# Top-k attention and a SmeLU MLP on one core: where ScalarE's copy of a chunk's MLP sum stands in the order

## The chip, the core and the metric

The kernel runs on one core of one Trainium2 chip. The metric is the device time of the whole program in microseconds (us): 1482.36 is the median of three runs, 1481.56 to 1483.75. The core's engines each have their own queue of instructions and work through it in order: TensorE (PE in the profile, with PEld for its weight loads), VectorE (DVE), ScalarE (ACT), GpSimd (POOL), and SyncE (SP), whose queue issues the transfers (DMA). Engines wait for one another by semaphores.

## The reference

Attention over 8 batches, 8 heads, 576 positions and head size 64, in which each row keeps only its 32 largest scores; its output goes, heads side by side, as 4608 rows of 512 into an MLP with 2048 hidden units.

```python
scores = scale * np.matmul(q, k.transpose(0, 1, 3, 2))
kth = np.partition(scores, -top_k, axis=-1)[..., -top_k:-top_k + 1]
scores = np.where(scores >= kth, scores, -1000000000.0)
attn = softmax(scores)                      # exp(scores - max) / (sum + 1e-09)
x = np.matmul(attn, v)                      # then (B,H,S,D) -> (B*S, H*D)

h = x @ w_in
g = np.where(h >= 1, h, np.where(h <= -1, 0.0, (h + 1) ** 2 / 4))
out = g @ w_out
```

All numbers are float32.

## The kernel before

**Attention in steps.** The work is cut into 144 steps; a step is 128 query rows of two heads. In a step TensorE makes the scores `sp` (line 358) and ScalarE copies them, scaled, to `s` (L359). VectorE finds the 32nd largest of each row: it folds the row in two halves, the pairwise larger and smaller ones (`more`, `less`, L372), and runs MAX8 and MATCH_REPLACE8 over them (L379 to L446); `kth` is the result (L451). ScalarE makes the exponentials `e` (L395) with the negated row maximum `nmax` (L393); VectorE masks and sums them (L458), and GpSimd divides them by their sum (L411, with VectorE's reciprocal `rz`, L404). The weights are then transposed: early and in the last steps by TensorE (`pw`, `pwt`, L473 and L479, with a diagonal matrix `diag` that ScalarE makes, L408), and in all other steps by way of DRAM: ScalarE splits the words into 16-bit `halves` (L488), SyncE writes them out as `rows` (L490) and a transposing transfer brings them back as `wT` (L492). TensorE multiplies with the values (`po`, L506 or L514) and ScalarE copies the outcome into `xT` (L519 or L521). Keys and queries are turned in the same two ways; on the way through DRAM ScalarE's part is `parts` (L283) and SyncE's are `lines<-parts` (L285) and a transposing transfer (L292).

**The MLP in chunks.** A chunk is 128 rows of `xT`; there are 36, one after every four steps, counted from 0 in what follows. For each chunk TensorE makes 8 hidden groups of 256 units (`ph`, L539, eight matrix products each; the last chunk has 16 groups of 128) and, from the activated `g`, 16 final products that are summed in one PSUM tile, `py` (L578). Of `py` there is one buffer, so the first final product of a chunk, which begins a new sum, has to wait until the old sum has been read. ScalarE makes `r` and `g` of each hidden group (L550, L558), and GpSimd finishes `g` (L565 to L568); in the last chunk VectorE does that (L554, L555). After the 16th final product ScalarE copies `py`, scaled, to `y` (L581) and SyncE sends `y` to the output (L583). In the profile each matrix product of the MLP shows as two records: a hidden group as 16, a final product as 2.

**Who sets the order.** The order of instructions on TensorE, VectorE, ScalarE and GpSimd is the order in which the program hands them out: a manual schedule is opened before the first step and closed after the last. Every step has 7 places (`slot`), in each of which VectorE's next part, and if they are due ScalarE's, GpSimd's and TensorE's other parts, are handed out. MLP work sits in a list `pending` and is taken by a budget of TensorE's time (`advance`, `take`). The last 8 final products of a chunk are put behind the first three hidden groups of the next. Two things are already handed out later than they are made: the readings of hidden groups (`reads`) and GpSimd's part of them (`bounds`). The order on SyncE is not written by hand; it is chosen when the program is built.

**Around a hand-over** from one chunk to the next, in nearly all chunks, TensorE has: the old chunk's last final product, three hidden groups of the new chunk, the new chunk's first final product, then scores and `po`. Before the change ScalarE has `y` straight after what was handed out before the last final product.

Of the kernel before, what the change touches and what calls it, by code (L numbers as in the profile page):

```python
# [11 lines left out]
F32 = mybir.dt.float32  # L12
# [14 lines left out]
def kernel(  # L27
# [10 lines left out]
    nc = tc.nc  # L38
# [3 lines left out]
    P = 128  # L42
# [134 lines left out]
    def run(ctx, paired):  # L177
# [352 lines left out]
        def mlp(xT, rows, pool, last):  # L530
            gs, group, whole_g = {}, 1 if last else GROUP, set()
            py = []

            def hidden(x):
                ph = ps.tile([P, group, P], F32, name="ph", tag="ph", bufs=3)
                for i in range(group):
                    f = x * group + i
                    for kk in range(NK):
                        nc.tensor.matmul(ph[:, i], w_in[:, kk, f * P:(f + 1) * P], xT[:, kk],  # L539
                                         start=(kk == 0), stop=(kk == NK - 1))  # L540

                reads.append(partial(read, x, ph))
                if not holding:
                    issue_reads()

            def read(x, ph):
                while len(bounds) > 1:
                    bounds.popleft()[1]()
                r = pool.tile([P, GROUP, P], F32, name="r", bufs=2)[:, 0:group]
                nc.scalar.activation(r, ph, AF.Relu, bias=half, scale=0.5 * unit)  # L550
                gs[x] = g = pool.tile([P, GROUP, P], F32, name="g", bufs=2 * LAG)[:, 0:group]
                if last:
                    nc.scalar.activation(g, ph, AF.Relu, bias=minus_half, scale=0.5 * unit)
                    nc.vector.scalar_tensor_tensor(out=r, in0=r, scalar=1.0, in1=r, op0=ALU.min, op1=ALU.mult)  # L554
                    nc.vector.tensor_tensor(out=g, in0=r, in1=g, op=ALU.add)  # L555
                    whole_g.add(x)
                    return
                nc.scalar.activation(g, ph, AF.Relu, bias=minus, scale=unit)  # L558
                by_act = converted < n_pieces and x % 2
                if by_act:  # L560
                    nc.scalar.activation(r, r, AF.Square)
                bounds.append((slots_done, partial(bound, x, r, g, by_act)))

            def bound(x, r, g, by_act):
                nc.gpsimd.tensor_scalar(r, r, 1.0, 0.0, ALU.min, ALU.max)  # L565
                if not by_act:
                    nc.gpsimd.tensor_tensor(out=r, in0=r, in1=r, op=ALU.mult)  # L567
                nc.gpsimd.tensor_tensor(out=g, in0=r, in1=g, op=ALU.add)  # L568
                whole_g.add(x)

            def final(f):
                if f == 0:
                    py.append(ps.tile([P, DM], F32, name="py", tag="py", bufs=1))
                if f // group not in gs:
                    issue_reads()
                while f // group not in whole_g:
                    bounds.popleft()[1]()
                nc.tensor.matmul(py[0], gs[f // group][:, f % group], w_out[:, f, :], start=(f == 0), stop=(f == NF - 1))  # L578
                if f == NF - 1:
                    y = (late or words).tile([P, DM], F32, name="y", bufs=1)  # L580
                    nc.scalar.activation(y, py[0], AF.Copy, scale=unit)  # L581
                    for p0, p1, dst in rows:
                        nc.sync.dma_start(out=dst, in_=y[p0:p1])  # L583

            behind = []
            while pending and pending[-1][3]:
                behind.insert(0, pending.pop())
            for x in range(NF // group + LAG):  # L590
                if x < NF // group:
                    pending.append((NK * group, needed(x * group + group - 1, False), partial(hidden, x), False))
                if x < LAG:
                    for _ in range(min(GROUP + 1, len(behind))):
                        pending.append(behind.pop(0)[0:3] + (False,))
                else:
                    for f in range((x - LAG) * group, (x - LAG + 1) * group):
                        pending.append((DM // P, needed(f, True), partial(final, f), x >= NF // group))
# [22 lines left out]
        total, spent = len(chunks) * (NK * NF + NF * DM // P), 0  # L621
        converted, inspected, due = 0, 0, 0.0

        reads, bounds, holding, slots_done = [], deque(), False, 0

        def issue_reads():
            while reads:
# [138 lines left out]
        for m in range(n + 2):  # L766
# [22 lines left out]
            for slot in range(SLOTS):  # L789
                now = start + (dve_time - start) * (slot + 1) / SLOTS  # L790
                for _ in range(parts[slot]):
                    next(top_k, None)
                if m < n and converted < n_pieces:
                    if slot in now_converting:
                        convert(now)
                elif slot == 3 and late is not None:
                    if m % 2:
                        inspect()
                    elif paired:
                        load(late, inspected, 1, 2)  # L800
                if slot == 1 and 1 <= m <= n and state[m - 1]["by_tensor"]:
                    pe_time = max(pe_time, done[m - 1] + 2.0) + 1.0
                    transpose_w(state[m - 1])
                    ready_at[m - 1] = pe_time + 1.8
                if slot == 3 and 1 <= m <= n and state[m - 1] is not None and not state[m - 1]["by_tensor"]:
                    move_w(state[m - 1])
                    ready_at[m - 1] = done[m - 1] + 15.0
                if slot == 3:
                    finish_turns()
                if slot == 2 and m == n and paired:  # L810
                    judge(ps, att)
                if slot == 2 and (early or m == first_late or m >= n - 1):
                    values_until(m)
                if m == 0 and slot in (1, 2):
                    next(first)
                holding = not early and m % 2 == 0 and slot in (1, 2) and m < n
                if slot == 2 and not early:
                    if m % 2 == 0:
                        while len(reads) < 3 and pending and taken is not None and taken.__name__ == "hidden" and take():
                            pass  # L820
                    begin_until(min(m + 2, len(state)))
                    holding = False
                    issue_reads()
                    values_until((m - 2) // 2 * 2)
                    begin_until(m + 3 - m % 2)
                if slot == 4 and early:
                    begin_at(m + 2)
                if slot == (6 if early else 1):
                    queries(m + (3 if early else 5))
                    if (m < n and prep is None and next_keys < B and steps[m][0] == next_keys - 1 and steps[m][1] >= 1  # L830
                            and (next_keys > 1 or converted == n_pieces)):
                        prep = (turned_keys_of if next_keys > 1 else keys_of)(next_keys)
                    if prep is not None and (m % 2 == 0 or next_keys == 1):
                        got = next(prep, None)
                        pe_time += 0.5 if next_keys < 2 else 0.0
                        if got is None:
                            prep, next_keys = None, next_keys + 1
                        else:
                            keys[next_keys] = got
                            value_loads = got.get("loads", value_loads)  # L840
                    elif value_loads is not None:
                        next(value_loads, None)
                if paired and early and spent == 0 and not pending:
                    rest = ps.tile([P, NT, P], F32, name="rest", tag="py", bufs=1)
                    for i in range(5):
                        nc.tensor.transpose(rest[:, i % NT, :], ident, ident)
                advance((EARLY_SHARE if early else share) / SLOTS if m < n else 32.0, now)
                slots_done += 1
                while bounds and (early or m >= n or bounds[0][0] < slots_done - 2):
                    bounds.popleft()[1]()  # L850
            for _ in (top_k if top_k is not None else ()):
                pass
        while pending:
            advance(32.0, pe_time + 8.0)
            while bounds:
                bounds.popleft()[1]()
        order.__exit__(None, None, None)


# [45 lines left out]
```

## Time and profile before

| What | Value |
|---|---|
| Median of the timed runs | 1482.36 us |
| Profiled execution: its time, its span | 1484.11 us, 1482.2 us |
| TensorE's clock granted, mean | 0.992 |
| TensorE busy | 1435.8 us, 97% |
| VectorE busy | 1403.9 us, 95% |
| ScalarE busy | 1158.0 us, 78% |
| GpSimd busy | 926.6 us, 63% |
| `y` (L581) | 36 times, 583 to 604 ns, median 597 |
| Transfer of `y` (L583) | 40 issues, to landing 3.7 us (median) |

The profile is of one execution, whose span is the time from its first to its last instruction; what lies around the span is the rest of its time. "Busy" counts time in which an engine works, not waits. In timelines each line has start, duration, engine, line of the kernel, operation, what it writes `<-` what it reads, and sizes; a bracket at the end gives the time for which the engine was idle just before, and what ended it. Ends of TensorE's products in the profile are modelled, so two that follow each other can overlap there by a tenth or two. VectorE's and GpSimd's durations contain whatever blocked them after their start.

### The profile page before, as it was taken

How to read it: one execution, taken by the hardware profiler on the slowest of the kernel's cores; microseconds unless marked ns; L12 is line 12 of the kernel's file. 1: busy time of each engine (PE TensorE's matmuls, PEld its weight loads, DVE VectorE, ACT ScalarE, POOL GpSimd, SP SyncE). 2: the span in 40 equal slices, each digit the busy share in tenths (PEclk: the TensorE clock that was granted, in tenths of full speed). 3: DMA queues.
4: the chain of work that ended last, by engine and by line, in shares of the span. 5: the costliest groups of instructions: out<-in, count | busy, mean ns of one | idle time of the engine just before them, and what ended most of it. 6: DMA issues, size and time to landing. Idle time of an engine off the chain costs nothing.

```text
span 1482.2 us, 32086 instructions
## 1 busy us (share of the span) xinstructions
PE 1435.8 (97%) x10755; PEld 1044.6 (70%) x10755; DVE 1403.9 (95%) x4392; ACT 1158.0 (78%) x2221; POOL 926.6 (63%) x1310
## 2 busy tenths in 40 slices
PE   6998899999999999999999999999999999999998
PEld 5766677777777777767777777677777777777675
DVE  6989999999999999999999999999999999999912
ACT  7987877878888887887778888788778888777632
POOL 3474566776676666566766677567666666666730
PEclk8999999999999999999999999999999999999999
DMA  8633657775677767787677787787677886665510
GB/s 252 196 121 107 177 152 203 196 194 162 167 206 204 193 193 205 193 209 174 163 195 203 196 198 194 195 214 183 174 197 187 202 202 167 168 166 142 149 25 17
DMA packets 510319, 260.94 MB, mean 176 GB/s; under 512 B 460992, under 2 KB 469184, under 8 KB 510144
## 3 DMA queue, kind: packets, MB, share of 16 engines
q1 hardware_dynamic: 510144, 258.80, 66.4%
q8 instruction: 87, 1.43, 0.4%
q14 instruction: 88, 0.72, 0.2%
HBM read 62.91 MB, written 102.63 MB: 112 GB/s over the span
## 4 chain that ended last, share of the span: by engine, by line
PE 80%; DVE 10%; DMA 4%; ACT 4%; issue 2%; SPq 1%; ACTq 0%; DVEq 0%
PE ph L539 30%; PE py L578 29%; PE sp L358 9%; PE po L506 9%; DVE more L379 2%; DMA rows<-halves 2%; DVE e L458 2%; DMA wT<-rows 1%; PE po L514 1%; DVE more L372 1%; DVE tops L420 1%; DVE tops L428 1%; DVE tops L392 1%; PE pw L473 1%; ACT halves L488 1%
## 5 line engine op out<-in xcount | busy, mean ns | idle before, releaser
L539 PEld LDWEIGHTS ph<-xT,w_in 128*128 128x128 f32 x4608 | 547.0, 192 | 102.6 <-issue 71.1
L539 PE MATMUL ph<-xT,w_in 128*128 128x128 f32 x4608 | 555.7, 276 | 2.3 <-ACT g L558 1.4
L578 PE MATMUL py<-w_out,g 128*128 128x512 f32 x1152 | 541.5, 597 | 1.8 <-ACT y L581 1.8
L565 POOL TENSOR_SCALAR r<-r 128x256 f32<-128x256 f32 x280 | 166.9, 596 | 413.4 <-ACT r L550 409.7
L379 DVE MATCH_REPLACE8 more<-tops,more 128x288 f32<-128x288 f32 x864 | 375.1, 437 | 0.0
L578 PEld LDWEIGHTS py<-w_out,g 128*128 128x128 f32 x1152 | 199.0, 191 | 166.5 <-issue 163.8
L488 ACT COPY halves<-e 128x1152 uint16<-128x1152 uint16 x268 | 293.6, 1143 | 18.5 <-DMA rows<-halves 18.1
L568 POOL TENSOR_TENSOR g<-r,g 128x256 f32<-128x256 f32 x280 | 241.6, 863 | 22.0
L458 DVE SCALAR_TENSOR_TENSOR e<-s,kth,e 128x577 f32<-128x577 f32 x288 | 246.9, 893 | 0.1
L411 POOL TENSOR_SCALAR e<-e,rz 128x576 f32<-128x576 f32 x268 | 235.9, 890 | 13.2 <-DVE rz L404 13.2
L395 ACT ACTIVATE e<-s,nmax 128x576 f32<-128x576 f32 x288 | 222.5, 773 | 4.7
L550 ACT ACTIVATE r<-ph,half 128x256 f32<-128x256 f32 (+1 forms) x296 | 136.1, 460 | 107.8 <-PE ph L539 99.7
L359 ACT ACTIVATE s<-sp 128x576 f32<-128x576 f32 x288 | 171.9, 649 | 61.7 <-PE sp L358 57.7
L567 POOL TENSOR_TENSOR r<-r 128x256 f32<-128x256 f32 x276 | 183.1, 663 | 23.0
L358 PE MATMUL sp<-kT,qT 64*128 64x288 f32 x1024 | 163.1, 436 | 8.3 <-ACT kT L261 6.1
L506 PE MATMUL po<-wT,v_in 128*64 128x128 f32 x2048 | 138.8, 277 | 8.0 <-DMA wT<-rows 4.6
L358 PEld LDWEIGHTS sp<-kT,qT 64*128 64x128 f32 x1024 | 90.0, 189 | 79.3 <-issue 37.2
L506 PEld LDWEIGHTS po<-wT,v_in 128*64 128x64 f32 x2048 | 113.6, 137 | 32.4 <-issue 10.3
L558 ACT ACTIVATE g<-ph,minus 128x256 f32<-128x256 f32 x280 | 130.4, 466 | 0.0
L372 DVE TENSOR_TENSOR more<-s 128x576 f32<-128x576 f32 x144 | 124.1, 862 | 6.0 <-ACT s L359 6.0
L420 DVE MAX8 tops<-more 128x8 f32<-128x288 f32 x288 | 125.4, 443 | 0.0
L372 DVE TENSOR_TENSOR less<-s 128x576 f32<-128x576 f32 x144 | 117.7, 817 | 0.0
(91 smaller groups left out, 1370.0 us busy)
## 6 DMA issues: line engine op xcount, KB each, us to landing
rows<-halves SPq DMA_DIRECT2D x134, 576.0 KB, 3.3
lines<-parts SPq DMA_DIRECT2D x48, 256.0 KB, 3.1
q_in<-in_q_dram SPq DMA_DIRECT2D x32, 256.0 KB, 3.8
v_in<-in_v_dram SPq DMA_DIRECT2D x32, 256.0 KB, 4.5
out_dram<-y SPq DMA_DIRECT2D x32, 256.0 KB, 3.9
raw<-in_moe_w_in_dram SPq DMA_DIRECT2D x32, 256.0 KB, 3.3
raw<-in_moe_w_out_dram SPq DMA_DIRECT2D x32, 256.0 KB, 3.5
kT<-in_moe_w_in_dram SPq DMA_DIRECT2D x8, 512.0 KB, 5.2
```

Of the source, the lines that this page charges most:

```text
L358: nc.tensor.matmul(*x, start=True, stop=True)
L372: nc.vector.tensor_tensor(out=x, in0=s[:, :, 0:SH], in1=s[:, :, SH:S], op=op)
L379: nc.vector.match_replace(out=st["rest"][:, i, :], in_to_replace=eight(st["tops"], i, r - 8), in_values=src[:, i, :], imm_value=LOWEST)
L395: nc.scalar.activation(e[:, i, :], s[:, i, :], AF.Exp, bias=nmax[:, i:i + 1])
L411: nc.gpsimd.tensor_scalar(st["e"][:, i, :], st["e"][:, i, :], rz[:, i:i + 1], 1.0, ALU.mult, ALU.mult)
L458: nc.vector.scalar_tensor_tensor(out=st["all"][1][:, i, :], in0=st["all"][0][:, i, :], scalar=last[i], in1=st["all"][1][:, i, :], op0=ALU. ...
L488: nc.scalar.copy(halves[:, :, i * S:(i + 1) * S], st["e"][:, i, :].bitcast(U16).rearrange("p (k t) -> p t k", t=2))
L506: nc.tensor.matmul(po[j * D:(j + 1) * D], v_in[:, h, c, :] if c < NT else v_tl[0][:, h, :], wT[:, block(j, c)], start=(c == 0), stop=(c == ...
L539: nc.tensor.matmul(ph[:, i], w_in[:, kk, f * P:(f + 1) * P], xT[:, kk], start=(kk == 0), stop=(kk == NK - 1))
L567: nc.gpsimd.tensor_tensor(out=r, in0=r, in1=r, op=ALU.mult)
L568: nc.gpsimd.tensor_tensor(out=g, in0=r, in1=g, op=ALU.add)
L578: nc.tensor.matmul(py[0], gs[f // group][:, f % group], w_out[:, f, :], start=(f == 0), stop=(f == NF - 1))
```

## The change

The copy to `y` and its transfer are no longer made in place by the last final product. They become a small function, `give`, that is put into a queue `outputs` together with the number of places so far (`slots_done`). The queue is emptied in three spots: at the end of a place, if an entry is more than three places old or the steps are over; in front of the first final product of the next chunk, if the entry is still there; and at the very end.

```diff
             def final(f):
                 if f == 0:
+                    while outputs:
+                        outputs.popleft()[1]()
                     py.append(ps.tile([P, DM], F32, name="py", tag="py", bufs=1))
...
                 if f == NF - 1:
-                    y = (late or words).tile([P, DM], F32, name="y", bufs=1)
-                    nc.scalar.activation(y, py[0], AF.Copy, scale=unit)
-                    for p0, p1, dst in rows:
-                        nc.sync.dma_start(out=dst, in_=y[p0:p1])
+                    outputs.append((slots_done, partial(give, py[0])))
+
+            def give(total):
+                y = (late or words).tile([P, DM], F32, name="y", bufs=1)
+                nc.scalar.activation(y, total, AF.Copy, scale=unit)
+                for p0, p1, dst in rows:
+                    nc.sync.dma_start(out=dst, in_=y[p0:p1])
...
-        reads, bounds, holding, slots_done = [], deque(), False, 0
+        reads, bounds, outputs, holding, slots_done = [], deque(), deque(), False, 0
...
                 slots_done += 1
+                while outputs and (m >= n or outputs[0][0] < slots_done - 3):
+                    outputs.popleft()[1]()
                 while bounds and (early or m >= n or bounds[0][0] < slots_done - 2):
                     bounds.popleft()[1]()
...
             advance(32.0, pe_time + 8.0)
             while bounds:
                 bounds.popleft()[1]()
+        while outputs:
+            outputs.popleft()[1]()
```

In the built program the orders of TensorE, VectorE and GpSimd are what they were; only `y` on ScalarE and the queue of SyncE differ. On ScalarE `y` now stands behind these instructions that it stood ahead of: in chunk 0, behind fifteen (two `diag`, three `wT`, the query and key copies, `xT`, four `s`); in chunks 1 to 7, behind `e`, `r`, `g`, `r`, `g`; in chunks 8 to 31, behind `nmax`, `e`, two passes over a piece of weights (L173), two `halves`, `e`, `r`, `g`; in chunk 32, behind the same without the two passes; in chunk 34, behind two pairs of `r` and `g`; in chunks 33 and 35 it has not moved. On SyncE the transfer of `y` stands behind the query transpose and one `raw` load, and in about half the chunks `rows<-halves` too, from chunk 8 on; in chunks 1 to 7 it has not moved.

## The prediction

> **What bounds the kernel now.** I read, in this order: the page's busy times, the chain that ended last, busy time by stretch, everything that touches `y` and `py`, and the instruction timelines of TensorE (PE) and ScalarE (ACT) around one hand-over.
>
> ```profile
> PE 1435.8 (97%) x10755; PEld 1044.6 (70%) x10755; DVE 1403.9 (95%) x4392; ACT 1158.0 (78%) x2221; POOL 926.6 (63%) x1310
> ...
> PE 80%; DVE 10%; DMA 4%; ACT 4%; issue 2%; SPq 1%; ACTq 0%; DVEq 0%
> ```
>
> Two engines are nearly full; ScalarE is not. Two neighbouring chunks, from one first final product to the next:
>
> ```profile
> core 0: us, PE busy (x) PEld busy (x) DVE busy (x) ACT busy (x) POOL busy (x), PEclk, DMA share, GB/s
> 1077.15:1114.92 37.77, 37.77 (x274) 27.29 (x273) 37.77 (x121) 30.10 (x59) 25.03 (x36) 1.00 0.79 199
> 1114.92:1152.70 37.78, 37.78 (x275) 27.30 (x274) 37.78 (x121) 31.05 (x60) 25.04 (x36) 1.00 0.74 183
> ```
>
> TensorE and VectorE both have no idle time, ScalarE has about 7 us a chunk. So an idle moment of ScalarE is worth nothing by itself, while a new stall of TensorE in such a chunk has no gap beside it to vanish into. Who waits around `y`:
>
> ```profile
>   PE py L578: 24.3, 27
> ...
> who waited for it (us, times):
>   PE py L578: 1.8, 1
> ```
>
> ScalarE waits 24.3 us in 27 places for the chunk's last final product; TensorE waits for the copy once, 1.8 us. Chunk 25 (the first is 0) in ScalarE's timeline (start, duration; the idle time before it in brackets), then TensorE's:
>
> ```profile
> 1108.42 0.47 ACT L558 ACTIVATE g<-ph,minus 128x256 f32<-128x256 f32 x1
> 1109.77 0.60 ACT L581 ACTIVATE y<-py 128x512 f32<-128x512 f32 x1 [0.88 <-PE py L578]
> 1110.26 0.20 ACT L393 ACTIVATE nmax<-tops 128x2 f32<-128x2 f32 x1
> ...
> 1115.12 0.46 ACT L550 ACTIVATE r<-ph,half 128x256 f32<-128x256 f32 x1
> 1115.47 0.46 ACT L558 ACTIVATE g<-ph,minus 128x256 f32<-128x256 f32 x1
> 1115.83 0.46 ACT L550 ACTIVATE r<-ph,half 128x256 f32<-128x256 f32 x1
> ```
> ```profile
> 1107.85 1.88 PE L578 MATMUL py<-w_out,g 128*128 128x512 f32 x4
> 1109.57 5.52 PE L539 MATMUL ph<-xT,w_in 128*128 128x128 f32 x48
> 1114.92 1.02 PE L578 MATMUL py<-w_out,g 128*128 128x512 f32 x2
> ```
>
> The old chunk's last final product ends at about 1109.7; three hidden groups (5.2 us) follow, then the next chunk's first final product at 1114.92, which overwrites `py` (one buffer) and so needs `y` done. Today `y` ends at 1110.37, 4.5 us early.
>
> **The skill.** "ScalarE: Activation LUTs", What ACT_TABLE_LOAD costs: an ACTIVATE without pointer operands takes 186 ns + 0.833 ns an element, and neighbours overlap by about 93 ns. For 512 elements that is 613 ns; the trace has 583 to 604, and the next one starts 0.49 after `y`. "TensorE: Matmul & The Clock Gate", Architectural detail: only weight loads are pulled ahead on TensorE, ScalarE is strictly first in, first out. The trace agrees: `nmax` stands behind `y`'s wait. "SBUF — State Buffer", two separate sides: VectorE's two-input operations and GpSimd exclude each other for a whole instruction. The trace agrees: `more`, 0.74 undisturbed, took 1.11 at 1123.60 under a GpSimd `g`.
>
> **The change, part by part.** The instruction orders of TensorE, VectorE and GpSimd are the same as before. Only `y` on ScalarE and SyncE's queue move.
>
> *Chunks 8 to 31.* `y` goes behind `nmax`, `e`, two sign passes, two `halves`, `e`, and one `r`, `g`. What is removed: its wait and its place. In chunk 25 `nmax` can start 0.37 after `g`, at 1108.79 (its `tops` ended at 1107.4), instead of 1110.26: ScalarE is 1.47 earlier. Then `y` starts where the second `r` stood less this, 1115.83 - 1.47 = 1114.36, and ends at 1114.96. TensorE's start after such an end: at chunk 1, where it waited, `y` ran 192.69 + 0.58 = 193.27 and the product started at 193.42, 0.15 later. So it starts at 1115.11, not 1114.92: a stall of 0.19 us that did not exist. Chunks 13 to 19 have a wait of 0.81 in place of 0.88, so 0.26. In chunks 8 to 11 `nmax` itself waited for VectorE (1.4 us after ScalarE was free), so nothing moves ahead and the sum is 461.98 + 0.60 + 0.15 = 462.73 against 460.93 in chunk 8: 1.8, until TensorE is that much later against VectorE; then 0.2 to 0.3.
>
> *Chunks 1 to 7.* `y` stood behind `halves` without a wait; now it stands behind `e`, `r`, `g`, `r`, `g`: 2.0 us later (chunk 7: 422.31 becomes 424.40, ending 424.99, and the product starts at 425.14, not 423.16). This stall is of phase: once TensorE runs 2 us later against VectorE and ScalarE, it does not recur.
>
> *Chunk 0.* ScalarE sat 2.91 us idle before `y` (121.79), with `diag` behind it; TensorE then waited 0.97 for `diag`, and VectorE 2.79 for scores at 130.94. Without `y` in front, this chain comes about 1.0 earlier: a gain of 1.0 for both. *Chunk 32*: covered, 1 us to spare. *Chunks 33 and 35*: not moved.
>
> *Chunk 34, in the tail.* `y` goes behind two `r`, `g` pairs of the last chunk's short groups, and the second `r` waits for TensorE itself (1452.51). Its `g` starts at 1452.77, `y` at 1453.03, ending 1453.63; the first final product starts at 1453.78 against 1452.31: 1.47, and from there to the end TensorE has no idle time. Lost in full.
>
> *SyncE.* The transfer of `y` moves past the query transpose, a `raw` load and, in about half the chunks, `rows<-halves`. Behind it then wait `rows<-halves` in the others: in chunk 25 it would issue at about 1115.7 instead of 1114.88. Its reader, the transpose at 1119.33, feeds products that show no wait there: nothing, and at worst 0.8 a chunk. Where `rows` comes first it issues up to 3 us earlier, and that too lands in slack.
>
> **The sum.** Cover exists: TensorE waits 1.34, 0.74 and 2.52 between 597 and 639, 1.95 and 0.69 at 945 and 967, and 2.13 + 0.93 + 0.79 between 1408 and 1422, all for work that descends from VectorE. Chunk 0: -1.0. Chunks 1 to 12: 2.0 of phase and some 1.3 of steady stalls against 4.6 of cover, but VectorE may be slowed with them (0 to +4): I take +1.0. Chunks 13 to 21: 8 x 0.26 = 2.1 against 2.6 of cover: +0.2. Chunks 22 to 31: 10 x 0.19 to 0.29 (the larger if `parts`' overlap isn't regained) = 1.9 to 2.9. VectorE's cycle there is 37.77 like TensorE's, because its `more` and `less` end by GpSimd's `r` and `g`, which come from TensorE; so it is paced and will follow, and the 2.13 at 1408 does not help: +2.4. Chunk 34: +1.5. Sum +4.1: the profiled span would be 1482.2 + 4.1 = 1486.3. The profiled execution took 1484.11, 1.9 around its span, and the median of the timed runs is 1482.36, which I use: 1486.5.
>
> What isn't shown is the answer of VectorE to GpSimd's moved `r` and `g` (up to 1.4 earlier). A step of VectorE is 9.14 at best and 9.55 on average, so about 0.4 x 128 steps = 52 us are such blocking. A change of a tenth is 5 us, either way.
>
> **Rivals.**
> 1. *The stalls fall into TensorE's own waits* (VectorE is the true bound and does not follow). Cover of 4.6, 2.6 and 3.85 swallows all up to 1422; left are -1.0 and +1.5, with some phase: 1483. For it: VectorE is not idle between 131 and 1410. Against: its cycle equals TensorE's to 0.01 in chunks 22 to 30.
> 2. *Faster, by less blocking.* GpSimd's first `r`, `g` after a hand-over come 1.4 earlier and leave `more`/`less` alone. It decides once VectorE's step loses more than 0.03 us (0.13 a chunk, 4 us over 32) and TensorE's waits shrink with it. They are some 12 us from 597 to 1422 and cap it; a third of that: 1478.5. Against: at 1114.39 to 1115.8 `more` and `less` run free today, just where the earlier GpSimd work would land.
> 3. *The 2 us does recur*, because VectorE falls back as far as TensorE in chunks 1 to 11: 7 x 2.0 + 4 x 1.8 = 21, less 4.6 to 10 of cover: +10 to +15, about 1495. Against: the wait is of phase.
>
> That the change does not do what it says is excluded: ScalarE's order shows it.
>
> **How the numbers follow.** Forecast, small loss: 0.48; rival 1: 0.25; rival 2: 0.14; rival 3: 0.13. No change is within 0.2%, or 3.0 us, about what this kernel's runs can tell: 1479.4 to 1485.3. The forecast's own range is 1483.5 to 1490, of which about an eighth lies under 1485.3. Slower 0.42 + 0.13 + 0.02 of rival 1 = 0.57; faster 0.13; the same 0.30. Range for 8 in 10: 1480 to 1493, leaving out half of rival 2 and most of rival 3.
>
> **What would show it.** ScalarE's wait for `py` before `y` gone in chunks 8 to 31; TensorE's waits for `y` some 25 to 33 instead of 1, of 0.2 to 0.3 us in the steady chunks (under 15 us in all); `pw` at about 121.7 without its 0.97; the first final product of chunk 35 waiting 1.4 to 1.5 for `y`; chunks 22 to 30 at 37.96 to 38.06. I am wrong if these stalls are absent (ScalarE earlier than worked out), if VectorE's mean step moves by more than 0.03, or if stalls of 2 us stay through chunks 1 to 11.

## The result and the profile after

The changed kernel took 1497.69 us (median of six runs, 1493.48 to 1499.85) against 1483.7 us (median of six, 1481.56 to 1486.86) for the kernel before: a ratio of 1.0091, with an interval of 1.0072 to 1.0109. It is slower, as forecast, but by 14 us, not by 4, and the time lies above the range of 1480 to 1493. The profiled execution took 1499.85 us with a span of 1497.8; before, the span was 1482.2. The difference to explain is therefore 15.6 us in the profile.

From the page of the kernel after: TensorE's and the others' busy times, the chain that ended last, and the group of the final products (busy time, mean ns | idle time before them and what ended it).

```profile
PE 1444.6 (96%) x10755; PEld 1049.5 (70%) x10755; DVE 1415.7 (95%) x4392; ACT 1158.1 (77%) x2221; POOL 922.5 (62%) x1310
...
PE 84%; ACT 7%; DMA 3%; DVE 3%; issue 2%; SPq 1%; POOL 0%; ACTq 0%; DVEq 0%; POOLq 0%
...
L580 PE MATMUL py<-w_out,g 128*128 128x512 f32 x1152 | 544.7, 599 | 14.1 <-ACT y L586 13.0
```

The number of instructions is the same. TensorE now stands still for 14.1 us in front of final products, nearly all of it for `y`. (The copy is L586 now and the final products L580.) What touches `y`, after:

```profile
L586 ACT ACTIVATE y<-py x36: 571/589/610, 132.0 to 1491.8; 128x512 f32<-128x512 f32 x36
its engine sat idle before it (us, times) until:
  issue: 3.7, 1
  PE py L580: 0.3, 1
who waited for it (us, times):
  PE py L580: 13.0, 8
  PEld py L580: 1.4, 1
```

The two waits have changed places. ScalarE's 24.3 us before `y` have become 0.3; TensorE's 1.8 us behind it have become 14.4 (13.0 and 1.4; PEld, the weight load, belongs to TensorE). The first was idle time of an engine that nobody waited for, the second is not.

How late the first final product of a chunk is, after less before, read from both timelines:

| First final product of chunk | Later by, us | Wait for `y` at this place in the record, us |
|---|---|---|
| 0 | 0.97 | none (no moved instruction stands ahead of it: two executions differ by this) |
| 1 | 3.62 | 0 |
| 2 | 5.85 | 3.02 (1.81 before) |
| 3 | 7.52 | 0 |
| 4, 5 | 8.75, 8.82 | 2.11, 0 |
| 6, 7, 8 | 9.88, 10.93, 11.99 | 0.82, 0.82, 0.83 |
| 12 | 13.28 | 0.07 to 0.10 in each of 9 to 12 |
| 13 | 14.84 | 2.17 |
| 14 | 11.46 | 0.09 |
| 21 | 13.64 | 0.01 to 0.09 in each of 14 to 21 |
| 22, 23 | 12.76, 12.09 | 2.08, 0.01 |
| 33 | 14.42 | 0.03 at most |
| 34, 35 | 14.23, 15.60 | 0, 1.20 |

Waits in the record are some 0.16 to 0.24 shorter than the stalls by start times, because ends of matrix products are modelled and overlap what follows. Busy time by stretch, after, for chunks 6 and 25, each from its first final product to the next chunk's:

```profile
core 0: us, PE busy (x) PEld busy (x) DVE busy (x) ACT busy (x) POOL busy (x), PEclk, DMA share, GB/s
357.49:396.32 38.83, 38.01 (x273) 27.37 (x273) 38.83 (x121) 30.06 (x58) 26.74 (x37) 1.00 0.59 162
1089.74:1127.76 38.02, 38.01 (x272) 27.36 (x273) 38.02 (x122) 30.04 (x59) 26.05 (x37) 1.00 0.72 195
```

Before, both took 37.77. TensorE's work in them is alike (38.01), and the difference of 0.82 is the wait. VectorE is busy for all of both, as it was before: its busy time simply grows with the window. A chunk from 5 to 7 costs over four times as much more (1.06) as a late one (0.25), and each of the three does. ScalarE's timeline in chunk 5 of the kernel after, and then TensorE's:

```profile
348.78 0.47 ACT L550 ACTIVATE r<-ph,half 128x256 f32<-128x256 f32 x1 [1.23 <-PE ph L539]
349.15 0.47 ACT L558 ACTIVATE g<-ph,minus 128x256 f32<-128x256 f32 x1
349.51 1.04 ACT L283 COPY parts<-q_in 128x1024 uint16<-128x1024 uint16 x1
350.44 0.21 ACT L393 ACTIVATE nmax<-tops 128x2 f32<-128x2 f32 x1
...
352.55 2.19 ACT L488 COPY halves<-e 128x1152 uint16<-128x1152 uint16 x2
354.64 0.77 ACT L395 ACTIVATE e<-s,nmax 128x576 f32<-128x576 f32 x1
...
356.39 0.47 ACT L558 ACTIVATE g<-ph,minus 128x256 f32<-128x256 f32 x1
356.75 0.60 ACT L586 ACTIVATE y<-py 128x512 f32<-128x512 f32 x1
```
```profile
351.15 5.52 PE L539 MATMUL ph<-xT,w_in 128*128 128x128 f32 x48
357.49 1.10 PE L580 MATMUL py<-w_out,g 128*128 128x512 f32 x2 [0.82 <-ACT y L586]
```

This is the part that comes back, and the prediction missed it: 3.2 us in chunks 5 to 7. The `r` at 348.78 waited for TensorE. From it to `y`, ScalarE has no idle time: nothing in between waits for VectorE or a transfer. `y` starts 7.97 after that `r`, lasts 0.60, and TensorE starts 0.14 later: 8.71. TensorE, without the wait, is due 7.73 after the same `r` (in the kernel before, 339.88 to 347.61). The gap of 0.98 is a loop of these two engines alone. If TensorE is late, the `r` is as late, so the next `y` is late by as much again. Nothing shifts against anything, and the stall comes back in each chunk. (The other 0.07 of each 1.05 follows at once: the two records of the first final product take 1.10 after the stall, against 1.02 in the kernel before.) The same holds far beyond these three. Of the chunks from 1 to 32, in all but 1, 3, 12 and 21 the last wait of ScalarE ahead of `y` is that of an `r` for TensorE; only the length of the loop differs.

In chunks 1 to 3 the loop is not what adds time. In chunk 1 the last wait ahead of `y` is `nmax`'s for VectorE (1.32 us at 192.24), in chunk 3 it is `halves`' for a `rows` transfer (2.07 us at 275.34), and the 1.67 of chunk 2 are no wait at all; they are the clock, below.

Two more stalls are not of the forecast size, those at chunks 13 and 22. ScalarE and SyncE of the kernel after, at the first of them:

```profile
624.33 2.21 ACT L488 COPY halves<-e 128x1152 uint16<-128x1152 uint16 x2 [1.95 <-DMA rows<-halves]
...
627.84 0.59 ACT L586 ACTIVATE y<-py 128x512 f32<-128x512 f32 x1
```
```profile
618.59 2.60 SPq L203 DMA_DIRECT2D v_tail<-in_v_dram  x4
621.28 0.55 SPq L490 DMA_DIRECT2D rows<-halves  x1
```

`halves` needs the buffer that an earlier `rows` transfer empties, and that transfer was issued behind four loads of `v_tail`. `halves` waits 1.95 us (in the kernel before 1.09, behind `y`), and `y`, which now stands behind it, hands the wait to TensorE. ScalarE's strict order, which "TensorE: Matmul & The Clock Gate", Architectural detail, in the Trainium skill states, is seen here at work: `py` had been complete for some 7 us.

In chunk 0 the forecast gain is a loss. ScalarE and TensorE of the kernel after, and last the same TensorE work in the kernel before:

```profile
138.61 0.54 ACT L173 ACTIVATE raw<-raw,tiny 128x256 f32<-128x256 f32 x1 [1.59 <-DMA raw<-in_moe_w_in_dram]
```
```profile
143.44 3.78 PE L539 MATMUL ph<-xT,w_in 128*128 128x128 f32 x16 [3.56 <-ACT g L558]
```
```profile
141.51 2.05 PE L539 MATMUL ph<-xT,w_in 128*128 128x128 f32 x16 [1.35 <-ACT g L558]
```

Before, this pass over a piece of weights (L173) ran at 136.71 without a wait, and TensorE's wait at this place was 1.35. The load of `raw` was issued at 129.12 before and at 135.74 after. With the transfer of `y` fifteen ScalarE instructions later, the build chose another order for SyncE, in which key loads and that transfer stand ahead of `raw`. The wait of `pw` for `diag` (0.97) did go, as forecast; it was worth less than what came.

The two TensorE lines show a second loss: the same 16 records take 3.78 us instead of 2.05. TensorE's granted clock (PEclk) was 0.50 from 142.0 to 148.9 in the kernel after, and 1.00 in that stretch before. The kernel after has such stretches of half clock also at 200.1 to 203.5 and 630.2 to 633.6; the kernel before has them at 639.5 to 642.9 and 946.7 to 950.1, where the kernel after has 1.00 (the first 101 us and the end, where both have some, left aside). An estimate, half of the time that TensorE was at work in them: 1.8 us of chunk 0's 2.65, 0.9 of chunk 1's 2.24, all of chunk 2's 1.67; later one more against two fewer, so 2.7 of the 15.6 us in all. These stretches came during or within 1.6 us of TensorE's waits of 3.56, 3.02 and 2.17, but none came at its waits of 3.34 (at 164.22), 2.11 and 2.08. So a stall can cost more than its length, and no run here shows when it does.

### The profile page after: what moved, and what is told of

It reads as the page before. It is cut to its first block, busy times and chain, and to the rows that moved or that the text cites. A ratio compares the mean times of both kernels' runs of the same rounds, so it can differ in the third digit from the quotient of the medians.

```text
span 1497.8 us, 32073 instructions
## 1 busy us (share of the span) xinstructions
PE 1444.6 (96%) x10755; PEld 1049.5 (70%) x10755; DVE 1415.7 (95%) x4392; ACT 1158.1 (77%) x2221; POOL 922.5 (62%) x1310
## 4 chain that ended last, share of the span: by engine, by line
PE 84%; ACT 7%; DMA 3%; DVE 3%; issue 2%; SPq 1%; POOL 0%; ACTq 0%; DVEq 0%; POOLq 0%
PE py L580 31%; PE ph L539 30%; PE sp L358 10%; PE po L506 9%; DMA rows<-halves 1%; PE pw L473 1%; ACT halves L488 1%; PE po L514 1%; ACT e L395 1%; DMA wT<-rows 1%; ACT s L359 1%; ACT units L147 1%; ACT r L550 1%; DVE more L379 1%; ACT g L558 1%
## 5 line engine op out<-in xcount | busy, mean ns | idle before, releaser
L580 PE MATMUL py<-w_out,g 128*128 128x512 f32 x1152 | 544.7, 599 | 14.1 <-ACT y L586 13.0
L580 PEld LDWEIGHTS py<-w_out,g 128*128 128x128 f32 x1152 | 198.9, 191 | 183.7 <-issue 166.9
L458 DVE SCALAR_TENSOR_TENSOR e<-s,kth,e 128x577 f32<-128x577 f32 x288 | 261.4, 942 | 0.8 <-ACT e L395 0.6
L568 POOL TENSOR_TENSOR g<-r,g 128x256 f32<-128x256 f32 x280 | 216.2, 772 | 22.0
L567 POOL TENSOR_TENSOR r<-r 128x256 f32<-128x256 f32 x276 | 191.7, 695 | 23.0
L372 DVE TENSOR_TENSOR more<-s 128x576 f32<-128x576 f32 x144 | 118.7, 824 | 8.0 <-ACT s L359 8.0
L420 DVE MAX8 tops<-more 128x8 f32<-128x288 f32 x288 | 125.4, 442 | 0.0
L392 DVE MAX8 tops<-more 128x8 f32<-128x288 f32 x288 | 116.4, 443 | 0.0
```

Of the source, the lines that this page charges most:

```text
L458: nc.vector.scalar_tensor_tensor(out=st["all"][1][:, i, :], in0=st["all"][0][:, i, :], scalar=last[i], in1=st["all"][1][:, i, :], op0=ALU. ...
```

## The experiments

The theory: TensorE sets the pace, so each stall at a first final product counts nearly in full, except where TensorE waits anyway; the size is set by how far down ScalarE's queue `y` stands, in a loop of the two engines. The rivals: VectorE is the bound; the loss comes through SyncE's changed queue; it comes through GpSimd and VectorE blocking each other more. TensorE's clock was not tried apart; where a trace shows it at work, this is said. All ratios are to the kernel before on the same chip, run beside the others. The copy is L589 or L583 in some of these kernels, as L586 is in the kernel after.

**Chunk 0 alone.** The diff, against the kernel after, with `ch` the chunk's number:

```diff
-                    outputs.append((slots_done, partial(give, py[0])))
+                    if ch == 0:
+                        outputs.append((slots_done, partial(give, py[0])))
+                    else:
+                        give(py[0])
...
```

> Only chunk 0's copy is handed out late; all others stand in place. Theory A (ScalarE's order stalls TensorE, and in chunk 0 SyncE's new order delays a raw load): the first final product of chunk 1 comes 2 to 3 us later than in the kernel before, after a wait of ScalarE for the raw load of about 1.6 us; total +1.5 to +3. Rival B (SyncE's queue does the damage wherever the transfer moves): the same here. Rival C (VectorE and GpSimd block each other more, all along): 0 +-1. My forecast had -1.0 for this part.

Measured: 1481.36 against 1479.36 us, 1.0014 [1.0001, 1.0027]: 2 us slower. The wait for `raw` at L173 is there (1.51 us). What follows: chunk 0's share is a loss, not the forecast gain of 1.0. The chunk itself is about 3 us late at its end, some 1.8 of it again at half clock (141.6 to 148.5); part of that is given back later, where TensorE's waits for other work, from chunk 12 to 14, are 1.38 us in all and not 4.68.

**Chunks 1 to 7 alone.** As above with `if 1 <= ch <= 7:`. SyncE's order is that of the kernel before.

> Only the copies of chunks 1 to 7 are late; SyncE's order is that of the kernel before throughout. Theory A: TensorE waits for y in these chunks as in the changed kernel, about 1 us in each of chunks 5 to 7 and 1 to 2 in chunks 1 to 3, 8 us by chunk 8; half or less of it is taken back by waits that TensorE had between 597 and 639; total +4 to +8. Rival B: 0, as SyncE's queue has not moved. Rival D (my forecast's step: a phase of 2 us, once): +1.

Measured: 1488.34 against 1479.36 us, 1.0057 [1.0042, 1.0072]: 9.0 us between the medians. The final products in its page:

```profile
L580 PE MATMUL py<-w_out,g 128*128 128x512 f32 x1152 | 542.5, 597 | 7.7 <-ACT y L589 7.7
```

Waits for `y` of 3.03, 2.20, 0.82, 0.83 and 0.81 us stand ahead of the first final products of chunks 2, 4, 6, 7 and 8: the five of the kernel after. TensorE gets 9.4 us late by chunk 8 (0.4 at chunk 1) and stays so through chunk 12. Of these 9 us, 3.2 are the loop in chunks 5 to 7, and an estimated 3.4 are half clock, at 160.2 to 163.6 (after a wait for a transfer, 2.98 us) and 276.3 to 279.7 (after the wait of 2.20). What it meets then, as the sum of all of TensorE's waits in the two stretches in which the prediction saw cover (those for `y` in brackets), and by how much TensorE gets nearer to the kernel before from the first to the last first final product of the stretch:

| Kernel | Chunk 12 to 14: waits, us | nearer by | Chunk 21 to 23: waits, us | nearer by |
|---|---|---|---|---|
| before | 4.68 (0) | | 2.64 (0) | |
| transfer alone (below) | 4.38 (0) | 2.06 | 2.28 (0) | 1.93 |
| chunks 1 to 7 alone | 2.25 (0) | 4.08 | 2.55 (0) | 1.67 |
| after | 2.76 (2.27) | 1.82 | 2.41 (2.08) | 1.55 |

So 9 us of lateness made 2.4 us of other waits vanish in the first stretch and about nothing in the second. In the kernel after nearly all of the other waits vanish, but its own stalls for `y` stand in their place: the waits shrink by 1.9 and 0.2. What TensorE makes up beyond its waits is clock: the half clock of the kernel before at 639.5 and 946.7 is absent in the two kernels between, and in the kernel after the one at 946.7 is gone while the one at 639.5 has its like at 630.2. The kernel with the transfer alone makes up 1.93 in the second stretch without being late by 9 us, so that part is not lateness taken in.

**Chunks 8 to 34 alone.** As above with `if ch >= 8:`.

> Only the copies from chunk 8 on are late. Theory A: 0.2 to 0.35 us a chunk in chunks 8 to 31 and 1.4 in chunk 34, less what waits at 597 to 639 and at 945 take in: total +3 to +6, chunks 23 to 30 at 37.95 to 38.05 us each. Rival B: more than half of the whole, +7 or more, as SyncE's order differs here most. Rival C: +5 to +10, with TensorE's waits for y under a third of it.

Measured: 1489.5 against 1479.36 us, 1.0062 [1.0047, 1.0076]: 9 to 10 us. It has a single wait of 1.61 at chunk 9 (the phase that the prediction has for chunk 8; it comes once), 0.31 a chunk in 9 to 12 and 14 to 21, waits of 3.35 and 2.14 at chunks 13 and 22, 0.24 a chunk from 23 on, and 1.20 at chunk 35. Here TensorE arrives at chunk 8 in time, so chunk 9's 1.61 is visible; in the kernel after it was already 12 us late there, and the same place cost 0.33.

**The two places with the transfer in front of `y`.** As above with `if ch in (12, 21):`.

> Only the copies of chunks 12 and 21 are late: y then stands behind two halves that wait for the transfer of the rows before. Theory A: TensorE waits 2 to 3.4 us for y after each of the two and does not make up, as it otherwise does there, what it is behind: total +2 to +5. If steady stalls of 0.3 us made the loss of the run with chunks 8 to 34, this is within 1 us of the kernel before.

Measured: 1481.17 us, 1.0009 [0.9996, 1.0022], against 1480.29 for the kernel before: less than expected. Both waits for `y` are in the trace, 2.25 and 2.01 us, but all waits of TensorE in the two stretches are 2.56 and 3.08 us, or 5.6 in all, where the kernel before has 7.3 and the one with the transfer alone 6.7. The new stalls took the place of old ones. By start times this holds for the first stretch; in the second this execution loses 2.4 us against the one with the transfer alone, 1.7 of it at half clock (962.0 to 965.4). Large in the record, the two are worth little in the median; the interval reaches from nothing to 3 us.

**The transfer alone.** The copy stays in place; only what sends `y` is queued:

```diff
-                    outputs.append((slots_done, partial(give, py[0])))
+                    y = (late or words).tile([P, DM], F32, name="y", bufs=1)
+                    nc.scalar.activation(y, py[0], AF.Copy, scale=unit)
+                    outputs.append((slots_done, partial(give, y)))
...
```

> The copy stands in place as before; only the transfer of y is handed out three places later, so that SyncE's queue gets another order. Theory A: within 2 us of the kernel before. Rival B: +5 to +13. No theory expects a wait of TensorE for y here beyond the one of the kernel before.

Measured: 1479.6 against 1479.36 us, 0.9997 [0.9988, 1.0007]. This does not settle the rival that blames SyncE's queue. Compared issue by issue over the 746 issues of each trace, SyncE's order here departs from that of the kernel before in 26 places and from that of the kernel after in 73, and in chunk 0 it is the old one. The one-place kernel below is the better test.

Against what was expected, TensorE waits for `y` four times: 0.88 in front of chunk 2, and 0.24 or 0.25 (0.45 to 0.48 by start times) in front of 6, 7 and 8. At these three the last wait ahead of `y` is `nmax`'s for VectorE (1.45 us each time), so a stall behind VectorE can come back too. The kernels with only chunk 0 late have the same three.

**Chunk 0 by two places in place of three.** As "chunk 0 alone", with `slots_done - 2` for `slots_done - 3`. SyncE then keeps `raw` between the key loads.

> Only chunk 0's y and its transfer are late, but by two places, so that SyncE still issues the load of raw between the k_in loads as in the kernel before. Theory (the loss of 2 us in chunk 0 came from raw being issued 6.6 us later): no wait for raw at ScalarE's pass on L173, and the time between 1 us less and 0.5 us more than before. Rival (it came from ScalarE's or VectorE's order in chunk 0): 2 us more, as with three places.

Measured: 1478.78 against 1479.54 us, 0.9992 [0.9982, 1.0002]. The pass at L173 no longer waits:

```profile
136.97 0.52 ACT L173 ACTIVATE raw<-raw,tiny 128x256 f32<-128x256 f32 x1
```

With `raw` issued at 132.24, 3.5 us earlier than in the kernel after, the loss is gone, though `y` still stands behind two `diag` and more. TensorE's wait is 1.35 us again, and no half clock follows it. So the late `raw`, and with it SyncE's order, is the likely cause in chunk 0, and the theory's -1 to +0.5 held; `y` itself moved too (behind ten instructions, not fifteen), so it is not the order alone that differs.

**One place instead of three**, in all chunks (`slots_done - 1` for `slots_done - 3`). `y` then stands behind three instructions in chunks 1 to 7, and behind six in 8 to 31.

> Handed out one place later instead of three. y stands behind e, r, g in chunks 1 to 7, behind nmax, e, two passes and two halves in chunks 8 to 31 (ahead of e, r, g), behind two r, g pairs in chunk 34; chunk 0 keeps SyncE's order and has y behind diag only. Theory A (TensorE loses what y ends later than its three hidden groups): no wait of TensorE for y in chunks 8 to 31 except about 0.8 us after chunks 12 and 21, where halves waits for a transfer; about 0.3 us in each of chunks 5 to 7; 1.2 to 1.4 after chunk 34; total +1 to +4. Rival B (SyncE's queue): +7 to +13, as SyncE's order differs from chunk 8 on as in the changed kernel. Rival C (blocking between VectorE and GpSimd): +5 or more, as the later r, g are earlier here too.

Measured: 1480.39 against 1480.29 us, 1.0003 [0.9993, 1.0013]. The waits shrink to 1.71 in front of chunk 2 (1.81 in the kernel before), 0.68 in front of 4, and 0.1 in chunks 5 to 7; in chunks 8 to 31 only the two behind `halves` are left (0.85 each), and chunk 34's 1.20. In chunks 5 to 7 `y` is two instructions (`r`, `g`, 0.71 us) further up ScalarE's queue and the wait is 0.7 shorter: the loop read backwards. The time is slightly better than expected: what remains fits into the cover. And two rivals fall here. SyncE's order is that of the kernel after everywhere but in chunk 0, where the rival had +7 to +13; and the later `r`, `g` are earlier here too, where the rival of VectorE and GpSimd had +5 or more.

**One place, in chunks 0 and 8 to 33 only** (1 to 7 and 34 in place): the best that these readings suggest.

> One place later in chunk 0 and in chunks 8 to 33 only; chunks 1 to 7 and 34 in place. Theory A: no new wait for y except 0.8 us after chunks 12 and 21, some 1 us gained at chunk 0 (diag no longer behind y): -2 to +1. Rival B: +5 to +9. Rival C: +3 or more.

Measured: 1481.15 against 1480.29 us, 1.0005 [0.9993, 1.0017]. No gain. ScalarE's wait before `y` has fallen from 24.3 us to 2.6, and nothing comes of it. TensorE waits for `y` in 11 places, 4.7 us in all: the expected ones in front of chunks 13 and 22 (1.40 and 0.39) and 0.78 in front of 2 (1.81 in the kernel before), but also some 0.25 in front of 9 to 12 and 18 to 20 and 0.38 in front of 21, which were not expected. No version tried beats the kernel before.

**TensorE made slower on purpose.** The kernel before, with the first final product of every chunk computed twice (the sum is begun anew, so the output is unchanged):

```diff
+                if f == 0:
+                    nc.tensor.matmul(py[0], gs[f // group][:, f % group], w_out[:, f, :], start=True, stop=True)
                 nc.tensor.matmul(py[0], gs[f // group][:, f % group], w_out[:, f, :], start=(f == 0), stop=(f == NF - 1))
```

> The kernel before with each chunk's first final product done twice (the second starts the sum anew), which gives TensorE 0.86 us more work at just the spot of the new wait, 36 times: 31 us. Theory A (TensorE sets the pace and VectorE follows it): +20 to +29, the rest taken in by TensorE's waits of some 12 us. Rival E (VectorE is the bound, TensorE's stalls fall into slack): +8 or less.

Measured: 1505.96 us, 1.0182 [1.0160, 1.0205], against 1480.29. That is 25.7 us for 36 x 0.86 = 31 us of added work: 83% is paid. The page's busy times, with TensorE at 1462.9:

```profile
PE 1462.9 (97%) x10827; PEld 1056.4 (70%) x10827; DVE 1421.0 (95%) x4392; ACT 1159.2 (77%) x2221; POOL 924.0 (62%) x1310
```

VectorE has the same 4392 instructions as ever and is busy for 17 us longer than before (1403.9), with no wait between 140 and 1420 us. A VectorE that set the pace would not have grown. The rival falls: TensorE is the bound, and VectorE keeps time with it.

**The kernel after, once more**, on the chip and beside the two-place and two-sum kernels:

> The kernel after the change, once more, beside the two following ones on one chip. Theory (the losses of the parts overlap, because time that TensorE has lost at one place covers the next stall): about +13 us, ratio 1.007 to 1.011, below the sum of the three parts measured apart (+2, +8.4 and +9.2). Rival (the parts simply add and the first comparison was lucky): +18 us or more.

Measured: 1495.65 against 1479.54 us, 1.0110 [1.0096, 1.0125], 16 us: the loss is confirmed. (This profiled execution has a span 5.2 us shorter than the first one of the same kernel; it has two stretches of half clock after the first 101 us, 143.7 to 147.2 and 198.4 to 201.8, or half as much time of it as the first.) The ratio is at the upper edge of the theory's, the 16 us lie between the two expectations. The three parts give 1.0014, 1.0057 and 1.0062, 1.33% together; with the intervals of each, that can't be told from 1.1%. That the parts overlap is seen at chunk 9 alone, and is not shown for the sum.

**Two sums.** With two PSUM tiles for the sum, a first final product no longer needs the `y` ahead of it. PSUM had room for this only with two instead of three tiles for the hidden products, which `po` shares. The same edit in the kernel before and in the one after:

```diff
-                ph = ps.tile([P, group, P], F32, name="ph", tag="ph", bufs=3)
+                ph = ps.tile([P, group, P], F32, name="ph", tag="ph", bufs=2)
...
-                    py.append(ps.tile([P, DM], F32, name="py", tag="py", bufs=1))
+                    py.append(ps.tile([P, DM], F32, name="py", tag="py", bufs=2))
...
```

> The kernel before with two PSUM tiles for the MLP sum, and two instead of three for the tile of the hidden products, which makes the room. It is only the partner of the next kernel: between 2 us less (final products never wait for y) and 15 us more (hidden products wait for their tile).

> The kernel after the change with the same two PSUM tiles for the MLP sum: the first final product of a chunk no longer needs the y of the chunk ahead. Theory (the loss is TensorE's wait for y at that product): no waits for y beyond 0.3 us in all, and at most 3 us more than its partner. Rival (the loss comes through other work displaced on VectorE, GpSimd or SyncE): 10 us or more above its partner, although no final product waits.

Measured: 1601.45 us for the first (1.0827 [1.0809, 1.0845]), far outside what was expected of it, and 1549.03 us for the second (1.0456 [1.0441, 1.0471]). The late copy is 52 us *faster* here. No final product waits for `y` in either. TensorE waits for `g` instead, at its third hidden group of a chunk, since that takes the tile of the first. The timelines around one such place, with the early copy:

```profile
1196.19 2.57 PE L539 MATMUL ph<-xT,w_in 128*128 128x128 f32 x16 [2.71 <-ACT g L558]
```

and with the late copy:

```profile
1206.57 2.05 PE L539 MATMUL ph<-xT,w_in 128*128 128x128 f32 x16 [1.21 <-ACT g L558]
```

The difference of the waits is 1.5 us, the 1.47 by which the prediction had ScalarE's next work come earlier once `y` and its wait are out of the way. So that gain exists. In the kernel as it is, with three tiles for hidden products, nobody waits for it. In the two profiled executions the late copy is 47.1 us shorter: TensorE's waits are 33.7 less, and the mean granted clock is 0.985 against 0.975, an estimated 16 us. What follows for the rivals: without the wait for `y` the move costs nothing here, which speaks against displaced work on VectorE, GpSimd or SyncE. It is no clean test, of size above all, because the bound has moved, by 8% in the partner.

## Why the prediction was wrong

By its own terms, against the profiled execution after:

| Term of the sum | Forecast | Found |
|---|---|---|
| Up to chunk 0's first final product | 0 | +0.97 (no moved instruction) |
| Chunk 0 | -1.0 | +2.65 |
| Chunks 1 to 12, with the cover at 597 to 639 | +1.0 | +7.84 |
| Chunks 13 to 21, with the cover at 945 and 967 | +0.2 | +0.63 |
| Chunks 22 to 32 | +2.4 | +2.33 |
| Chunk 34 and the end | +1.5 | +1.19 |
| Sum | +4.1 | +15.6 |

**The step that failed: "This stall is of phase ... it does not recur".** The 2.0 us was worked out rightly for chunk 7 in the kernel before, where `nmax` waits 0.94 us for VectorE ahead of `y`. In the kernel after, a wait of this kind stands last ahead of `y` in chunk 1 alone; that such stalls do not recur is not shown, since the kernel with the transfer alone has one in three chunks running. The other half hangs on an `r` that waits for TensorE itself, and it comes back, in each of chunks 5 to 7 with nearly the same length. The same addition made on chunk 5 of the kernel before, where ScalarE waits for nothing but TensorE, gives it: five instructions move ahead of `y`, so `y` can start at 347.83 and TensorE at 348.58, against 347.61. That is 0.97, and 0.98 was found. For chunks 8 to 11 the prediction looked for just this remainder ("then 0.2 to 0.3"); for chunks 1 to 7 it did not. Chunks 1 to 7 alone built up 9 us, where it had 2.0, and in the whole change they built up 8.37 (3.62 to 11.99): 3.16 in chunks 5 to 7, by the loop; 2.24 in chunk 1, of which 1.2 are the longer wait for `y` and some 0.9 the clock; 1.67 in chunk 2, all clock; 1.23 in chunk 3, where `y` stands behind a `halves` that waits for a transfer. So "once" failed in three ways, and the loop is the one that repeats. The clock had no term in the sum: it is read from the trace, and no run varies it alone.

**"4.6 of cover" and "2.6 of cover" were counted in full.** The waits are where the prediction said, but by start times TensorE made up, net, 1.82 and 1.55 there; its waits shrank by 1.9 and 0.2, and the rest of the 1.55 is the half clock at 946.7 that did not come. Chunk 12's and chunk 21's own stalls, which it had at 0.26 each, stand where other waits vanished. The term of chunks 1 to 12 is then 9.66 built up (3.62 to 13.28 in the table of the result) less 1.82.

**Chunk 0 was wrong in sign.** The wait of `pw` went, as the step says. For SyncE, "nothing, and at worst 0.8 a chunk" did not look at what the new order does to the load of `raw` there. TensorE's wait for the hidden group grew from 1.35 to 3.56, behind a wait for that load, and an estimated 1.8 of half clock came on top. With two places in place of three the wait is 1.35 again, and no half clock follows it.

**Chunks 12 and 21**: 0.26 forecast for each, and waits of 2.17 and 2.08 found, behind `halves`. Alone they cost 0.9 us between the medians, with an interval that includes nothing.

**What was right.** Chunks 22 to 31 at 0.19 to 0.29 each, where 0.24 to 0.26 was found, and 13 to 19 at 0.26, where it was 0.32. Chunk 34 at 1.47, where 1.37 was found. That ScalarE's 24 us of waiting were worth nothing (the one-place kernels). That SyncE's queue costs nothing in general (the one-place kernel, with the order of the kernel after from chunk 1 on). That VectorE "is paced and will follow": the mark set for being wrong, a mean step of VectorE that moves by more than 0.03 us, was reached (from the starts of `kth`, steps 8 to 140: 9.545 before, 9.649 after), but it can't tell cause from effect, since TensorE's doubled product alone takes it to 9.679.

**The rivals.** The third had about the right time (1495, and a chance of 0.13) and the right place, but in part another cause: VectorE need not fall back for the stall to recur. Its closeness is in part luck: it counts 2.0 in each of seven chunks, and 21 less 4.6 to 10 is 11 to 16, not 10 to 15. (In the forecast, 2.1 against 2.6 of cover is entered as +0.2, with no working shown.) The first, a VectorE that does not follow, falls with the doubled product. For the second no run speaks: none is faster than the kernel before by more than its interval.

## What to carry to other kernels

Before a stall is put down to phase, follow the waiting instruction's queue back to the last wait in it. If that wait is for the very engine that will be stalled, the two form a loop, and the stall comes back in every round at the length of the loop less the round, as in chunks 5 to 7 here. A wait for a third engine is no proof of the contrary; do this for each stretch, since another instruction may be last in each. A wait that is removed from an engine with idle time is worth what somebody waits for it: here 1.5 us a chunk with two tiles for hidden products, and nothing with three. And a stall's length in the record is not its price: two of 2 us cost little by themselves because TensorE waits near there anyway, while 0.25 us in a chunk without any slack is paid each time. It can also be more than the record says: look at the granted clock behind a long stall, and compare it between the two traces before a difference is put down to waits.

## What the runs showed of the hardware

VectorE can show no idle time without being the bound. In the run with the doubled product it never waits between 140 and 1420 us, and its masked sum (L458) takes 972 ns on average, against 893 before and 878 in the kernel with the transfer alone, with the same instruction and sizes; over 288 of them this is 27 us between the last two, about the time added. It follows TensorE by longer instructions, not by gaps, so "busy 95%" and "no idle" did not mark it as a bound. That the stretch comes from GpSimd, which works on what TensorE delivers and which the prediction has blocking VectorE, is argued from its reading of one `more`, and was not tried apart.

TensorE's granted clock went from 1.00 to 0.50 for single stretches of 3.4 us or multiples of it, and the same kernel has them at other places in another execution. They go with the scatter of the times: of the 19 runs of the kernel before beside the last kernels, the nine with a mean granted clock of 0.993 have a median of 1479.0 us, the five with 0.991 one of 1481.2.
